# Attention, routed experts and a gated convolution FFN on one core: the first batch's rows and the late flag are taken earlier

## The chip, the core and the metric

The kernel runs on one core of one Trainium2 chip. The metric is the device time of one execution in microseconds (us), lower is better. An execution is timed as a whole; one execution is recorded by the hardware profiler, and its span (first to last instruction) is a little shorter than its own time.

## What is computed

Three stages, all in float32; the outputs of one are the inputs of the next.

```python
def reference(q_l, k_l, v_l, q_g, k_g, v_g, moe_*, moe2_*):
    # attention: 4 batches, 8 heads, 512 local rows with a window of 32, 32 global rows
    x = attention(...)                       # [4, 544, 512]
    # routed experts: 8 of them, one per row
    for b in range(4):
        for s in range(544):
            e = argmax(x[b, s] @ w_gate) or the row before's expert, by a local gate
            p = softmax(x[b, s] @ w_gate)
            y[b, s] = p[e] * (relu(x[b, s] @ w1[e]) @ w2[e])      # 512 -> 1024 -> 512
    # second FFN: 512 -> 1024, convolution of 3 taps along s, gate, 1024 -> 512
    h = relu(y @ w_in)
    c = conv3(h, conv_w)
    out = (h * sigmoid(c)) @ w_out
```

## The kernel before

**Stages.** The attention comes first. Its rows go to DRAM (`x_dram`), and the router sorts them by expert. The routed part then works in *slots*: slot `s` is up to 128 rows of one expert, gathered from `x_dram` by an indirect DMA and scattered to `y_dram` by another. 22 slots run: 0 and 1 in `fill`, 2 to 20 in `Moe.step` (L1280), 21 in `Moe.last` (L1190). Three more slots exist for other inputs, in a branch behind the last. The second FFN (`Ffn2.run`) then reads `y_dram` batch by batch, 8 units (blocks of 128 hidden columns) per batch.

**Arithmetic.** Every float32 factor is split into a high part and a low part, and each product is three matmuls: high x high, high x low, low x high. ScalarE makes the high part, VectorE subtracts it to get the low part. For activations these are `hi_t` (L1078/L1079: four transposes on TensorE, then the ScalarE copy) and `lo_t` (L1083); the tiles are `xh`/`xl` ahead of a first layer and `gh`/`gl` ahead of a second. For weights it is `Weights.split_k` (L1026/L1027: `wh`, `wl`). The weights of a slot's expert are split only where the expert changes (`resplit`, an `If` on a register).

**Order inside a step.** `step(s)` puts on TensorE: first layer of slot `s`, transposes of the rows `xs` of slot `s + 1`, second layer of slot `s - 1` (`l2_mm`, L1106), transposes of the hidden rows `hs` of slot `s`. Then `step(s + 1)` begins with its first layer (`l1_mm`, L1090). On VectorE: `xl`, the conversion of a piece of the second FFN's weights that is under way (`conv64`, L993 to L1000), the split of slot `s + 1`'s first-layer weights if its expert is new, the two `gl` of slot `s`, the split of second-layer weights if due. Every transpose group writes a PSUM buffer of the tag `tr`, of which there are two; so do `cwp` (L1166, transposed convolution weights) and `lf` (L946, the count behind the late flag). A buffer is free for the next group when its last reader is done, which for `hi_t` is `lo_t` on VectorE. Each engine takes its instructions in the order of the program.

**The end of the routed part.** `last(21)` mixes the first and second layers of the last slots with the split of the second FFN's input weights `W.f` (into the first-layer weight tiles), the loads of batch 0's rows (`load0`, L1331: five DMAs), their scaling by the router's probability (`scale0`, L1339) and transposes (`xt0`, L1346 to L1349), and ends with slot 21's copy from PSUM (L1259) and its scatter (L1063). Behind it every engine reads a flag into a register (L1178) and branches on it (L1179). The flag is not zero where a row of batch 0 lies in a slot so late that `load0` came before its scatter, or where more than 22 slots are needed; the branch then runs what is missing and loads, scales and transposes batch 0 again. Behind the branch the output weights are split and the second FFN starts.

**The second FFN's start.** TensorE's first layer of unit 0 and 1 (L1414), ScalarE's relu `f_hp` (L1438), convolution taps on ScalarE and VectorE (`fc`, L1431/L1433), gate (`fg`, L1449). Meanwhile SyncE loads rows of batch 1 (L1364: the global rows, then four times 128), which need all scatters; ScalarE scales the first 128 of them (L1370) in its order ahead of unit 1's `f_hp`.

```python
            rt.late_tokens(NSLOT - 4)            # L1685: NSLOT is 25
...
    def late_flag(self, n, t):                   # L944
        nc, f = self.nc, self.esi[:, 4, 1:2]
        nc.tensor.matmul(t, self.late, self.c.ones[:, 0:1], start=True, stop=True)
        nc.vector.tensor_scalar(f, self.esi[:, 4, 0:1], n - NA, None, ALU.is_gt)
        nc.vector.tensor_tensor(f, t, f, ALU.add)
```

Of the kernel before, what the change touches and what calls it, by code (L numbers as in the profile page):

```python
# [8 lines left out]
F32 = mybir.dt.float32  # L9
# [3 lines left out]
AF = mybir.ActivationFunctionType  # L13
ALU = mybir.AluOpType
# [3 lines left out]
P = 128  # L18
# [540 lines left out]
NSLOT = 25  # L559
NA = 2  # L560
# [413 lines left out]
SPLIT_W2 = {33: (0, 1, 2), 34: (3, 4, 5), 35: (6, 7)}  # L974
FILL = {1: 1, 3: 1, 6: 3, 7: 1, 8: 3, 9: 1, 10: 1, 11: 1, 12: 2, 13: 3, 15: 5, 16: 8}
HALF = 5
K_LAST = 2
N_GLOB = 6
N_GS = 4
N_Y = 24  # L980
PREP_F = ((3, 4, 5, 6), (1, 3, 5, 6), (1, 3, 5, 6))
PREP0 = {0: (0, 1, 12, 13), 3: (5, 2), 4: (6, 3), 5: (7, 4), 6: (8,), 7: (9,)}
POOL_L = ()
POOL_F = ()
DVE_F = (1, 3, 5, 7)
POOL_K = {1: (), 2: ()}


def conv64(nc, raw, out):
    hi, lo = raw[:, :, 1], raw[:, :, 0]  # L990
    v = nc.vector
    a = out.bitcast(I32)
    v.tensor_scalar(a, hi, 3, 0x7FFFFFFF, ALU.logical_shift_left, ALU.bitwise_and)  # L993
    v.scalar_tensor_tensor(a, hi, -2 ** 31, a, ALU.bitwise_and, ALU.bitwise_or)
    v.tensor_scalar(hi, hi, 1, 21, ALU.logical_shift_left, ALU.logical_shift_right)
    v.tensor_scalar(hi, hi, 897.0, -1.0, ALU.is_ge, ALU.mult)
    v.scalar_tensor_tensor(a, lo, 29, a, ALU.logical_shift_right, ALU.bitwise_or)
    v.tensor_scalar(lo, lo, 28, 1, ALU.logical_shift_right, ALU.bitwise_and)  # L998
    nc.gpsimd.tensor_tensor(a, a, lo, ALU.add)  # L999
    return lambda: v.scalar_tensor_tensor(a, a, 0x40000000, hi, ALU.bitwise_xor, ALU.bitwise_and)  # L1000


class Weights:
# [24 lines left out]

    def split(self, n, src, eng=None):
        for k in range(len(self.t[n])):  # L1030
            self.split_k(n, src, k, eng or (self.nc.gpsimd if k in POOL_K[n] else self.nc.vector))


class Moe:
# [134 lines left out]
    def run(self, cw6, cwr, cw, f2):  # L1169
        nc, W, tc = self.nc, self.W, self.tc  # L1170
        n = NSLOT - 3
        self.f2 = f2
        for s in range(NA, n - 1):
            self.step(s)
            if s == NA + 17:
                self.conv.append(conv64(nc, cw6, cwr))
        self.last(n - 1, cwr, cw)
        r = nc.values_load(self.rt.esi[0:1, 4, 1:2], min_val=0, max_val=P + 1)  # L1178
        with tc.If(r != 0):  # L1179
            r = nc.values_load(self.rt.esi[0:1, 4, 0:1], min_val=0, max_val=NB)  # L1180
            with tc.If(r > n - NA):
                for s in range(n, NSLOT):
                    self.slot(s)
                W.split(1, W.f)
            f2.load0()
            for i in range(5):
                f2.scale0(i, self.ps)
                f2.xt0(i, self.ps)
        for k in range(NFC):
            W.split_k(2, W.f, k, nc.gpsimd if k in POOL_F else nc.vector, nc.vector if k in DVE_F else None)  # L1190

    def last(self, s, cwr, cw):
        nc, W, f2 = self.nc, self.W, self.f2
        hp, hs = self.h_tile(), self.tp.tile([P, FF], F32, tag="hs", name="hs")
        xt, ht = self.xt.pop(s), {}
        w, y = W.t[1], {}
        ht = tuple(self.tp.tile([P, NFC, P], F32R, tag="g" + x, name="g" + x) for x in "hl")

        def split(a, b):
            for k in range(a, b):  # L1200
                W.split_k(1, W.f, k, nc.gpsimd if k in POOL_K[1] else nc.vector)

        def resplit(a, b):
            with self.tc.If(self.chg[s] != 0):
                for k in range(a, b):
                    W.split_k(2, W.s, k, nc.gpsimd if k in POOL_L else nc.vector)

        for k in range(K_LAST):
            self.l1_mm(xt, w, hp, k, range(2))
        split(0, K_LAST)  # L1210
        nc.scalar.activation(self.sig, self.sig, AF.Sigmoid)
        self.out(s - 1, self.l2(self.ht.pop(s - 1), W.t[2]))
        f2.load0()
        resplit(0, 4)
        for k in range(K_LAST, NKC - 1):
            self.l1_mm(xt, w, hp, k, range(2))
        self.conv_w(cwr, cw)
        self.rt.late_flag(s + 1, self.ps.tile([P, 4, P], F32, tag="tr", name="lf")[0:1, 0, 0:1])
        t = []
        for c in range(2):  # L1220
            self.l1_mm(xt, w, hp, NKC - 1, (c,))
            self.relu_c(hp, hs, c)
        for a in (0, 4):
            t.append(self.hi_t(hs, ht, a, self.ps))
        for a in (0, 4):
            self.lo_t(ht, a, t[a // 4])
        resplit(4, NFC)
        yp = self.y_tile()
        for k in range(NFC):
            self.l2_mm(ht, W.t[2], yp, k)  # L1230
            for f in PREP0.get(k, ()):
                if f < 10:
                    (f2.scale0 if f < 5 else f2.xt0)(f % 5, self.ps)
                else:
                    split(f - 10, f - 9)
        self.out(s, yp)

    def slot(self, s):
        nc, W = self.nc, self.W
# [37 lines left out]
        with self.tc.If(self.chg[s] != 0):  # L1277
            self.W.split(n, self.W.s, eng)

    def step(self, s):  # L1280
        W, hi = self.W, NSLOT - 3
        if NA < s <= NA + 16:
            self.raw_load(s - NA - 1)
        hs = self.relu(self.l1(self.xt.pop(s), W.t[1]))
        if s + 3 < hi:
            self.xs[s + 3] = self.gather(s + 3)
        self.xt[s + 1] = self.hi_lo_t(self.xs.pop(s + 1), NKC, "x")
        while self.conv:
            self.conv.pop()()
        self.resplit(s + 1, 1)  # L1290
        if s + 2 < hi:
            self.fetch(s + 1, 1)
        if s == NA:
            for _ in self.rest:
                pass
        else:
            self.out(s - 1, self.l2(self.ht.pop(s - 1), W.t[2]))
        self.ht[s] = self.hi_lo_t(hs, NFC, "g")
        self.resplit(s, 2)
        self.fetch(s, 2)  # L1300
        if NA < s <= NA + 16:
            self.convert(s - NA - 1)
# [15 lines left out]
class Ffn2:  # L1318
# [14 lines left out]
    def part0(self, i):  # L1333
        return (SG, 0, GT, 4) if i == 0 else (P, SG + P * i - P, i - 1, i - 1)

    def scale0(self, i, ps):
        n, _, j, a = self.part0(i)
        x = self.x_in[a][0:n]
        self.nc.vector.tensor_scalar(x, x, self.gate[0:n, j:j + 1], None, ALU.mult)  # L1339
# [227 lines left out]
def moe_kernel(ctx, tc, q_l, k_l, v_l, q_g, k_g, v_g, w_gate, w_local, w1, w2, w_in, conv_w, w_out, out):  # L1567
    nc = tc.nc
    outf = out.rearrange("b s d -> (b s) d")
    with tc.manual_schedule():  # L1570
# [90 lines left out]
        m, W, fill = todo["m"], todo["m"].W, todo["fill"]  # L1661
        xp = ctx.enter_context(tc.tile_pool(name="f_xp", bufs=1, reuse_waits="tile"))
        f2 = Ffn2(tc, xp, ident, y_dram, rt.gate, cw, W.t[1], W.t[2], outf)
        W.stage1(moe_ctx.enter_context(tc.tile_pool(name="w_y", bufs=1, reuse_waits="tile")))
        m.open(moe_ctx)
        with ExitStack() as c2:
            rp = c2.enter_context(tc.tile_pool(name="r_tb", bufs=1))
            rs = c2.enter_context(tc.tile_pool(name="r_ps", bufs=1, space=PSUM))
            m.fetch(0, 1)
            for i, y in enumerate(rt.phase_b(rp, lambda shape, name: rs.tile(shape, F32, tag="rt", name=name))):  # L1670
                if y == "idx":
                    for s in range(NA, NA + 3):
# [12 lines left out]
            rt.late_tokens(NSLOT - 4)  # L1685
        xa.close()
        W.ffn(moe_ctx.enter_context(tc.tile_pool(name="w_f", bufs=1)))
        m.run(cw6, cwr, cw, f2)
# [34 lines left out]
```

## Time and profile before

| | |
|---|---|
| three runs | 646.09, 648.47, 649.37 us; median 648.47 |
| the profiled execution | 645.35 us, its span 643.6 us |
| mean granted clock of TensorE | 0.995 of 2.4 GHz |
| busy in the span | TensorE 604.7 us (94%), VectorE 418.8 (65%), ScalarE 320.9 (50%), POOL 174.7 (27%) |

How to read the rows further down: PE is TensorE, DVE is VectorE, ACT is ScalarE, POOL is GpSimd, SP is SyncE; a "q" or "ld" behind the name is the engine's sequencer, or TensorE's weight loads. Times are us from the span's start unless marked ns. A timeline row has start, duration, engine, line, operation, output<-inputs, sizes, and how many like instructions it joins (x8); in brackets stands how long the engine sat idle before it and what released it. Matmuls are pipelined: the next one starts before the modelled end of the last.

### The profile page before, as it was taken

The page shows a single profiled execution, that of the slowest core. Times are in us where ns is not written, and L with a number is a line of the kernel's source. Part 1 is how long each engine was busy: PE and PEld are TensorE (multiplying, and loading weights), DVE is VectorE, ACT ScalarE, POOL GpSimd, SP SyncE. Part 2 cuts the span into 40 slices and gives each one's busy share as a digit, 9 for nine tenths or more (in the row PEclk, how much of TensorE's full clock was granted, in tenths as well). Part 3 has the DMA queues.
Part 4 walks back from the last instruction along what each step waited for, and adds up shares of the span by engine and source line. Part 5 has one row for each costly group of instructions (what it writes and reads, how often), then busy time and mean ns, then how long its engine had stood idle before and what let it go on. Part 6 is the DMA issues. An engine that isn't in the chain of part 4 may idle for free. (4 is left out here: it accounts for less than half of the span.)

```text
span 643.6 us, 15270 instructions
## 1 busy us (share of the span) xinstructions
PE 604.7 (94%) x5898; PEld 508.0 (79%) x5898; DVE 418.8 (65%) x874; ACT 320.9 (50%) x629; POOL 174.7 (27%) x226
## 2 busy tenths in 40 slices
PE   8888898888999999999999999987999999999997
PEld 7666676665778888888888888857998898898986
DVE  7877577958836676875778677586893393393340
ACT  4754555573225546352454634664874374373331
POOL 7664810070212232423222251000042042300200
PEclk9999999999999999999999999997999999999999
DMA  9999668652158454953545494023101201000001
GB/s 226 217 244 236 177 142 209 240 168 75 55 201 314 140 182 171 344 207 132 211 143 184 145 347 157 16 86 88 31 20 49 68 16 50 34 1 34 34 34 49
DMA packets 60089, 88.12 MB, mean 137 GB/s; under 512 B 25710, under 2 KB 34182, under 8 KB 59976
## 3 DMA queue, kind: packets, MB, share of 16 engines
q1 hardware_dynamic: 56488, 76.83, 38.3%
q0 software_dynamic: 3520, 10.23, 4.6%
q8 instruction: 48, 0.79, 0.5%
q14 instruction: 33, 0.27, 0.1%
HBM read 125.87 MB, written 15.79 MB: 220 GB/s over the span
## 5 line engine op out<-in xcount | busy, mean ns | idle before, releaser
L1433 DVE SCALAR_TENSOR_TENSOR fc<-f_hp,cw,fc 128x544 f32<-128x544 f32 (+2 forms) x66 | 51.4, 778 | 71.5 <-ACT fc L1431 70.0
L1027 DVE TENSOR_TENSOR wl<-ws,wh 128x512 fp32r<-128x512 f32 (+1 forms) x92 | 71.8, 848 | 5.3 <-ACT wh L1026 5.2
L1106 PE MATMUL yp<-wh,gh 128*128 128x512 f32 x176 | 71.0, 404 | 1.1 <-ACTq L1277 0.9
L1106 PE MATMUL yp<-wl,gh 128*128 128x512 f32 x176 | 69.0, 392 | 0.7 <-DVEq L1277 0.7
L1106 PE MATMUL yp<-wh,gl 128*128 128x512 f32 x176 | 69.1, 393 | 0.0
L1026 ACT CAST wh<-ws 128x512 fp32r<-128x512 f32 (+1 forms) x96 | 66.1, 779 | 0.0
L1255 ACT ACTIVATE hs<-hp 128x512 f32<-128x512 f32 x44 | 24.3, 595 | 74.2 <-PE hp L1090 74.1
L1090 PE MATMUL hp<-wh,xh 128*128 128x512 f32 x176 | 58.6, 405 | 0.7 <-ACT xh L1079 0.7
L1090 PE MATMUL hp<-wl,xh 128*128 128x512 f32 x176 | 56.2, 392 | 0.0
L1090 PE MATMUL hp<-wh,xl 128*128 128x512 f32 x176 | 56.0, 391 | 0.0
L1491 PE MATMUL f<-wh,fh 128*128 128x512 f32 (+1 forms) x144 | 55.5, 385 | 0.0
L1491 PE MATMUL f<-wl,fh 128*128 128x512 f32 (+1 forms) x144 | 55.0, 382 | 0.0
L1491 PE MATMUL f<-wh,fl 128*128 128x512 f32 (+1 forms) x144 | 55.0, 382 | 0.0
L1063 POOL DMA_INDIRECT y_dram<-ys,sidx x22 | 24.6, 1118 | 105.7 <-ACT ys L1259 88.9
L1083 DVE TENSOR_TENSOR gl<-hlp,gh 128x512 fp32r<-128x512 f32 x44 | 28.4, 686 | 32.4 <-ACT gh L1079 32.3
L278 ACT ACTIVATE pr<-sp,nm 128x128 f32<-128x128 f32 x128 | 36.6, 376 | 25.7 <-DVE nm L275 25.7
L999 POOL TENSOR_TENSOR wf<-wf,fx 128x512 int32<-128x512 int32 x16 | 20.8, 1303 | 100.9 <-DVE fx L998 100.9
L1259 ACT COPY ys<-yp 128x512 f32<-128x512 f32 x22 | 12.9, 587 | 61.2 <-PE yp L1106 56.5
L1051 POOL DMA_INDIRECT xs<-x_dram,gidx x22 | 27.5, 1249 | 45.5 <-ACT pr L278 34.0
L1106 PEld LDWEIGHTS yp<-wh,gh 128*128 128x128 f32 x176 | 33.1, 188 | 7.7 <-ACTq L1277 1.1
L1090 PEld LDWEIGHTS hp<-wl,xh 128*128 128x128 f32 x176 | 32.9, 188 | 7.8 <-DVE wl L1027 0.9
L1106 PEld LDWEIGHTS yp<-wh,gl 128*128 128x128 f32 x176 | 33.0, 188 | 7.6 <-DVE gl L1083 0.6
(357 smaller groups left out, 1492.5 us busy)
## 6 DMA issues: line engine op xcount, KB each, us to landing
ws<-in_moe_w_dram SPq DMA_DIRECT2D x42, 2048.0 KB
fx<-y_dram SPq DMA_DIRECT2D x17, 256.0 KB
raw<-in_k_l_dram SPq DMA_DIRECT2D x16, 256.0 KB
x_dram<-x SPq DMA_DIRECT2D x16, 256.0 KB
fx<-in_moe_w_in_dram SPq DMA_DIRECT2D x8, 512.0 KB
fx<-in_moe_w_out_dram SPq DMA_DIRECT2D x8, 512.0 KB
out_dram<-fy SPq DMA_DIRECT2D x16, 256.0 KB
VA<-in_v_l_dram SPq DMA_DIRECT2D x20, 192.0 KB
```

Of the source, the lines that this page charges most:

```text
L278: nc.scalar.activation(pr[:, hp, :], sp[:, hp, :], AF.Exp, bias=nm[:, hp:hp + 1], scale=-1.0)
L999: nc.gpsimd.tensor_tensor(a, a, lo, ALU.add)
L1026: (cp.tensor_copy if cp else self.nc.scalar.copy)(h, src[n][:, k, :])
L1027: eng.tensor_tensor(l, src[n][:, k, :], h.bitcast(F32), ALU.subtract)
L1051: self.nc.gpsimd.indirect_dma_start(out=xs, out_offset=None, in_=self.x_dram[0:n, :], in_offset=bass.IndirectOffsetOnAxis(ap=self.rt.gidx[ ...
L1063: self.nc.gpsimd.indirect_dma_start(out=self.y_dram[:, :], out_offset=bass.IndirectOffsetOnAxis(ap=self.rt.sidx[:, s:s + 1], axis=0), in_= ...
L1083: self.nc.vector.tensor_tensor(hl[1][:, a:a + 4], t, hl[0][:, a:a + 4].bitcast(F32), ALU.subtract)
L1090: self.nc.tensor.matmul(hp[c], a[:, k, :], b[:, 512 * c:512 * c + 512], start=k == 0 and m == 0, stop=k == NKC - 1 and m == 2)
L1106: self.nc.tensor.matmul(yp, a[:, k, :], b, start=k == 0 and m == 0, stop=k == NFC - 1 and m == 2)
L1255: self.nc.scalar.activation(hs[:, 512 * c:512 * c + 512], hp[c], AF.Relu)
L1433: nc.vector.scalar_tensor_tensor(c[:, a:b], hp[:, a + t:b + t], self.cw[:, t, f:f + 1], c[:, a:b], ALU.mult, ALU.add)
L1491: self.nc.tensor.matmul(yp[:, cs], x[:, c], w[:, cs], start=f == 0 and n == 0, stop=f == NFC - 1 and n == 2)
```

## The change

The rows of batch 0 in slots 19 and later now count as late (21 and later before). So `load0` goes out at the start of step 20, behind slot 18's scatter, instead of behind slot 20's second layer. The five `scale0` stand in front of `last`, the five `xt0` inside slot 21's first layer instead of its second. In `last` the first layer runs in one piece, the second layer of slot 20 holds the transposes of slot 21's hidden rows, and slot 20's copy stands behind the split of slot 21's second-layer weights. The late flag is computed behind step 17, as are the registers behind step 18; a second value (flag not zero) goes to TensorE's sequencer as a hint on where the branch will go. The convolution weights are converted one step earlier and transposed in step 20 instead of the last slot. Slot 21's result is copied into a buffer of the second FFN, and its scatter stands behind the branch (and once inside it).

```diff
-            self.step(s)
-            if s == NA + 17:
+            if s == n - 2:
+                f2.load0()
+            self.step(s, (cwr, cw) if s == n - 2 else None)
+            if s == NA + 15:
+                self.rt.late_flag(n, self.ps.tile([P, 4, P], F32, tag="tr", name="lf")[0:1, 0, 0:1])
+                f = self.rt.esi[:, 4, 1:3]
+                nc.vector.tensor_scalar(f[:, 1:2], f[:, 0:1], 0, None, ALU.not_equal)
+            if s == NA + 16:
+                self.flag = nc.values_load(f[0:1, 0:1], min_val=0, max_val=P + 1)
+                self.hint = nc.values_load(f[0:1, 1:2], engines=[mybir.EngineType.PE], min_val=0, max_val=1)
                 self.conv.append(conv64(nc, cw6, cwr))
-        self.last(n - 1, cwr, cw)
-        r = nc.values_load(self.rt.esi[0:1, 4, 1:2], min_val=0, max_val=P + 1)
-        with tc.If(r != 0):
+        for i in range(5):
+            f2.scale0(i)
+        y = self.last(n - 1)
+        with tc.If(self.flag != 0, label="late"):
+            self.scatter(n - 1, y)
+            nc.vector.memset(self.rt.sidx[:, n - 1:n], 4 * P * NT)
             r = nc.values_load(self.rt.esi[0:1, 4, 0:1], min_val=0, max_val=NB)
...
+        self.scatter(n - 1, y)
         for k in range(NFC):
...
-    def last(self, s, cwr, cw):
+    def last(self, s):
         nc, W, f2 = self.nc, self.W, self.f2
...
+        for k in range(NKC):
+            self.l1_mm(xt, W.t[1], hp, k, range(2))
+            for i in PREP0[k]:
+                f2.xt0(i, self.ps)
...
+        for c in range(2):
+            self.relu_c(hp, hs, c)
+        for k in range(2):
+            W.split_k(1, W.f, k, v)
...
+        yp, hp = self.y_tile(), self.ht.pop(s - 1)
         for k in range(NFC):
...
+            self.l2_mm(hp, W.t[2], yp, k)
+            if k in (1, 2):
+                t = self.hi_t(hs, ht, 4 * k - 4, self.ps)
+                self.lo_t(ht, 4 * k - 4, t)
+        with self.tc.If(self.chg[s] != 0):
+            W.split(2, W.s, v)
+        self.out(s - 1, yp)
+        for k in range(2, NKC):
+            W.split_k(1, W.f, k, v)
+        self.tc.mark_branch_hint_location("late", self.hint, engines=[mybir.EngineType.PE])
+        yp = self.l2(ht, W.t[2])
+        y = f2.x_in[3]
+        nc.scalar.copy(y, yp)
+        return y
...
-    def step(self, s):
+    def step(self, s, cw=None):
...
-            self.out(s - 1, self.l2(self.ht.pop(s - 1), W.t[2]))
+            yp, ht = self.y_tile(), self.ht.pop(s - 1)
+            for k in range(NFC):
+                self.l2_mm(ht, W.t[2], yp, k)
+                if k == 3 and cw:
+                    self.conv_w(*cw)
+            self.out(s - 1, yp)
...
-            rt.late_tokens(NSLOT - 4)
+            rt.late_tokens(NSLOT - 6)
```

`PREP0` is now `((), (0, 1), (2,), (3, 4))`: which `xt0` follow which quarter of the first layer. Lines shift a little by the change; in the three pieces below the changed kernel's L1074 is L1078 of before, L1079 is L1083, L1086 is L1090, L1102 is L1106, L1023 is L1027, L1059 is L1063 and L1271 is L1277.

TensorE from the end of step 17 into the first layer of slot 18, before:

```order
L1106 MATMUL yp<-wh_7_2746,gh 128x512
L1106 MATMUL yp<-wl_7_2747,gh 128x512
L1106 MATMUL yp<-wh_7_2746,gl 128x512
L1078 MATMUL hlp<-ident,hs 128x128 x8
L1277 UNCONDITIONAL_BRANCH
L1090 MATMUL hp<-wh_0_2724,xh 128x512 x2
L1090 MATMUL hp<-wl_0_2725,xh 128x512 x2
```

and with the change:

```order
L1102 MATMUL yp<-wh_7_2746,gl 128x512
L1074 MATMUL hlp<-ident,hs 128x128 x8
L1271 UNCONDITIONAL_BRANCH
L946 LDWEIGHTS late
L946 MATMUL lf<-c_ones,late 1x1
L1086 MATMUL hp<-wh_0_2724,xh 128x512 x2
L1086 MATMUL hp<-wl_0_2725,xh 128x512 x2
```

The count `lf` now stands between the transposes of slot 17's hidden rows and the first layer of slot 18; it stood in the last slot. Its buffer is that of the first four transposes.

VectorE in step 20, from the split of slot 21's first-layer weights on, with the change:

```order
L1271 COMPARE_AND_BRANCH
L1023 TENSOR_TENSOR wl_0_2725<-ws_3452,wh_0_2724 128x1024
L1023 TENSOR_TENSOR wl_1_2727<-ws_3452,wh_1_2726 128x1024
L1023 TENSOR_TENSOR wl_2_2729<-ws_3452,wh_2_2728 128x1024
L1023 TENSOR_TENSOR wl_3_2731<-ws_3452,wh_3_2730 128x1024
L1271 UNCONDITIONAL_BRANCH x2
L1163 COPY cw<-cwp 128x24
L1079 TENSOR_TENSOR gl<-hlp,gh 128x512 x2
```

The copy of `cwp` is new here; before, `gl` followed the four `wl` directly. In step 17 the same four `wl` (of slot 18) stand ahead of the two `gl` in both kernels.

POOL from slot 20's scatter to the second FFN, with the change:

```order
L1059 DMA y_dram<-ys,sidx 2176x512
L1184 COMPARE_AND_BRANCH
L1059 DMA y_dram<-fx,sidx 2176x512
...
L1184 UNCONDITIONAL_BRANCH
L1184 ISA
L1184 UNCONDITIONAL_BRANCH
L1059 DMA y_dram<-fx,sidx 2176x512
L1356 MEMSET f_hp_7519 128x1
```

L1184 is the branch on the flag; its two upper rows of `fx` are inside it and behind it. Before, both scatters stood ahead of the branch.

## Rows read from the trace of the kernel before

**Rows 1.** part 2 of the page: granted clock in 40 slices
```profile
PEclk9999999999999999999999999997999999999999
```

**Rows 2.** waits of TensorE, 371 to 466 us: total, times, longest
```profile
PE f L1414 <- PEq L1179: 4.2, 1, 4.2
...
PE f_tr L1379 <- DVE fxl L1381: 0.9, 1, 0.9
```

**Rows 3.** TensorE's timeline, end of step 17: start, duration, what
```profile
371.80 1.04 PE L1078 MATMUL hlp<-ident,hs 128*128 128x128 f32 x8
372.59 0.72 PE L1090 MATMUL hp<-wh,xh 128*128 128x512 f32 x2
```

**Rows 4.** VectorE's timeline, the same place
```profile
372.06 4.62 DVE L1027 TENSOR_TENSOR wl<-ws,wh 128x1024 fp32r<-128x1024 f32 x4
376.60 1.28 DVE L1083 TENSOR_TENSOR gl<-hlp,gh 128x512 fp32r<-128x512 f32 x2
```

**Rows 5.** two stretches: us, busy by engine, then the granted clock
```profile
437.12:443.95 6.83, 5.68 (x25) 5.71 (x26) 5.12 (x10) 2.18 (x4) 0.28 (x6) 0.50 0.55 145
443.95:447.10 3.15, 3.15 (x27) 3.15 (x26) 2.87 (x5) 2.11 (x4) 0.00 (x0) 1.00 0.39 120
```

**Rows 6.** TensorE's timeline, end of step 20 to the branch
```profile
409.75 0.72 PE L1090 MATMUL hp<-wh,xh 128*128 128x512 f32 x2
...
412.60 0.39 PE L1106 MATMUL yp<-wh,gh 128*128 128x512 f32 x1
...
418.04 0.62 PE L1090 MATMUL hp<-wh,xh 128*128 128x512 f32 x2
...
419.66 0.16 PE L946 MATMUL lf<-c_ones,late 128*1 128x1 bf16 x1
...
428.75 0.60 PE L1346 MATMUL f_tr<-ident,fx 128*128 128x128 f32 x4
...
433.40 0.63 PE L1346 MATMUL f_tr<-ident,fx 128*128 128x128 f32 x4
```

**Rows 7.** VectorE's timeline: step 20, last slot, after the branch
```profile
405.60 4.63 DVE L1027 TENSOR_TENSOR wl<-ws,wh 128x1024 fp32r<-128x1024 f32 x4
...
414.02 1.23 DVE L1027 TENSOR_TENSOR wl<-wf,wh 128x1024 fp32r<-128x1024 f32 x1 [0.15 <-ACT wh L1026]
...
424.60 2.49 DVE L1027 TENSOR_TENSOR wl<-ws,wh 128x512 fp32r<-128x512 f32 x4
...
438.73 0.69 DVE L1027 TENSOR_TENSOR wl<-wf,wh 128x512 fp32r<-128x512 f32 x1 [3.36 <-ACT wh L1026]
...
445.61 1.69 DVE L1433 SCALAR_TENSOR_TENSOR fc<-f_hp,cw,fc 128x544 f32<-128x544 f32 x2
```

**Rows 8.** ScalarE's timeline, last slot's copy and second FFN
```profile
434.55 0.59 ACT L1259 COPY ys<-yp 128x512 f32<-128x512 f32 x1
...
445.71 0.73 ACT L1370 ACTIVATE fx<-fx,gate 128x512 f32<-128x512 f32 x1 [0.21 <-DMA fx<-y_dram]
447.10 0.63 ACT L1438 ACTIVATE f_hp<-f 128x544 f32<-128x544 f32 x1 [0.66 <-PE f L1414]
```

**Rows 9.** POOL's timeline, the scatters of slots 20 and 21
```profile
419.10 0.97 POOL L1063 DMA_INDIRECT y_dram<-ys,sidx  x1 [8.00 <-ACT ys L1259]
435.41 0.97 POOL L1063 DMA_INDIRECT y_dram<-ys,sidx  x1 [15.34 <-DVE f_x0l L1349]
```

**Rows 10.** SyncE's timeline, the two loads of y rows
```profile
422.59 2.23 SPq L1331 DMA_DIRECT2D fx<-y_dram  x5
438.09 2.84 SPq L1364 DMA_DIRECT2D fx<-y_dram  x5
```

**Rows 11.** the branch behind the last slot, TensorE's sequencer, ns
```profile
L1179 PEldq COMPARE_BRANCH  x1: 3768/3768/3768, 434.1 to 434.1; - x1
```

**Rows 12.** chain that ended last, by time, 433 to 466 us
```profile
438.27 8.80 PE f L1414 x48
...
464.75 0.66 PE f_tr L1379 x4
```

More of the change, by code (lines that the diff above doesn't have):

```diff
@@ L976 @@
 HALF = 5
-K_LAST = 2
 N_GLOB = 6
@@ L981 @@
 PREP_F = ((3, 4, 5, 6), (1, 3, 5, 6), (1, 3, 5, 6))
-PREP0 = {0: (0, 1, 12, 13), 3: (5, 2), 4: (6, 3), 5: (7, 4), 6: (8,), 7: (9,)}
-POOL_L = ()
-POOL_F = ()
+PREP0 = ((), (0, 1), (2,), (3, 4))
 DVE_F = (1, 3, 5, 7)
-POOL_K = {1: (), 2: ()}
 def conv64(nc, raw, out):
@@ L1030, in split @@
         for k in range(len(self.t[n])):
-            self.split_k(n, src, k, eng or (self.nc.gpsimd if k in POOL_K[n] else self.nc.vector))
+            self.split_k(n, src, k, eng or self.nc.vector)
 class Moe:
@@ L1186, in run @@
             for i in range(5):
-                f2.scale0(i, self.ps)
+                f2.scale0(i)
                 f2.xt0(i, self.ps)
+        self.scatter(n - 1, y)
         for k in range(NFC):
-            W.split_k(2, W.f, k, nc.gpsimd if k in POOL_F else nc.vector, nc.vector if k in DVE_F else None)
-    def last(self, s, cwr, cw):
+            W.split_k(2, W.f, k, nc.vector, nc.vector if k in DVE_F else None)
+    def last(self, s):
         nc, W, f2 = self.nc, self.W, self.f2
-        hp, hs = self.h_tile(), self.tp.tile([P, FF], F32, tag="hs", name="hs")
-        xt, ht = self.xt.pop(s), {}
-        w, y = W.t[1], {}
-        ht = tuple(self.tp.tile([P, NFC, P], F32R, tag="g" + x, name="g" + x) for x in "hl")
[L1199 to L1211, printed above, removed]
-        self.out(s - 1, self.l2(self.ht.pop(s - 1), W.t[2]))
[L1213 to L1228, printed above, removed]
-        for k in range(NFC):
[L1230 to L1236, printed above, removed]
@@ new lines, in last @@
+        v = nc.vector
+        nc.scalar.activation(self.sig, self.sig, AF.Sigmoid)
+        xt, hp = self.xt.pop(s), self.h_tile()
+        for k in range(NKC):
+            self.l1_mm(xt, W.t[1], hp, k, range(2))
+            for i in PREP0[k]:
+                f2.xt0(i, self.ps)
+        hs = self.tp.tile([P, FF], F32, tag="hs", name="hs")
+        for c in range(2):
+            self.relu_c(hp, hs, c)
+        for k in range(2):
+            W.split_k(1, W.f, k, v)
+        ht = tuple(self.tp.tile([P, NFC, P], F32R, tag="g" + x, name="g" + x) for x in "hl")
@@ L1296, in step @@
         else:
-            self.out(s - 1, self.l2(self.ht.pop(s - 1), W.t[2]))
+            yp, ht = self.y_tile(), self.ht.pop(s - 1)
[4 more added lines that the diff above has]
+            self.out(s - 1, yp)
         self.ht[s] = self.hi_lo_t(hs, NFC, "g")
@@ L1334, in part0, with scale0 @@
         return (SG, 0, GT, 4) if i == 0 else (P, SG + P * i - P, i - 1, i - 1)
-    def scale0(self, i, ps):
+    def scale0(self, i):
         n, _, j, a = self.part0(i)
```

## The prediction

> **What bounds the kernel now.** I read the clock line first, then the waits of TensorE, then the timelines of each engine around every place the diff touches, and last the chain of waits. The clock line is full in every slice but one, the 28th [rows 1]. From 371 to 466 us TensorE waits for others little: its two stops that matter are 4.24 us in front of the second FFN and 0.88 us in front of the transposes at 464.75 us [rows 2, 12]. So through the routed slots the kernel lasts as long as TensorE's own instructions. What any of them waits is added to the end, unless a later wait of TensorE shrinks by as much.
>
> Around the branch it is otherwise. TensorE's matmuls of the last slot end at 434.03 us (433.40 + 0.63), and the next matmul is the second FFN's at 438.27 [rows 6, 12]. Behind that gap the clock is 0.50 (1.2 GHz) from 437.12 to 443.95: 25 matmuls are busy for 5.68 us there, where 27 take 3.15 right behind it [rows 5]. At full clock 25 would take 25/27 x 3.15 = 2.92 us, so the fall costs 2.8. The chain then runs through 48 matmuls in 8.80 us and ScalarE's `f_hp` of the second unit at 447.10 into a loop of ScalarE and VectorE, which releases TensorE's transposes at 464.75; from there TensorE sets the end [rows 8, 12]. What is gained at that 447.10 comes out at the end.
>
> **Step 17, the flag's early matmul: +4.8 us.** The matmul `lf` itself is cheap (0.16 us [rows 6]). Its place is not. It now stands on TensorE behind the eight transposes of `hs` and ahead of the first layer of slot 18. It takes the next buffer of the transposes' PSUM pair, which is free only when VectorE has made the first `gl` from it. In step 17 VectorE stands at another job: slot 18 starts a new expert, and the four `wl` of its first-layer weights run from 372.06 to 376.68; `gl` follows at 376.60, two in 1.28, so the first is done at 376.60 + 0.64 = 377.24 [rows 4]. Before, nothing on TensorE waited for this: the first layer began at 372.59, straight behind the transposes [rows 3]. TensorE takes its matmuls in order, so slot 18's first layer and all behind it now start at about 377.24 + 0.16 = 377.4, which is 4.8 us late. VectorE has no other work that fills this later, and TensorE has no wait from here to slot 20 that could shrink.
>
> A page of the Trainium skill, "TensorE: Matmul & The Clock Gate" (section "Architectural detail"), says that TensorE's queue can pull weight loads ahead of matmuls in flight. If that held for matmuls, the stall would be nothing and the time 644.8; it is said of weight loads only, and no row here shows a matmul that passed a waiting one.
>
> **The clock in step 17: +2.8 us, or nothing.** From the end of the transposes (371.80 + 1.04 = 372.84 [rows 3]) to 377.24 TensorE idles 4.4 us. The trace has one idle of that length, 4.24 us, and the clock fell; idles of 0.9 us show no fall [rows 1, 2]. So I take the fall, at the 2.8 us worked out above. It may not come, since TensorE was dense ahead of this gap: lower end 0. If the half clock lasts as long as it did and all of it is work, it costs half of 6.83 = 3.4 us [rows 5]: upper end.
>
> **Step 20, the conv weights' transpose: +1.2 us, inside the next term.** `cwp` takes one of the same two buffers, so the second four transposes of `hs` wait until VectorE has copied it out, and that copy stands behind the four `wl` that end at 405.60 + 4.63 = 410.23 [rows 7]. Slot 21's first layer then starts at about 410.95 instead of 409.75 [rows 6].
>
> **The last slot and the start of the second FFN: -3.7 us.** Worked from before's own durations, without the shift of step 17. First layer: 2 x (412.60 - 409.75) = 5.70. Five groups of input transposes, one small: about 5 x 0.35 = 1.77 (four in 0.36 by 428.75 to 429.11, where the next matmul starts). Second layer of slot 20: 418.04 - 412.60 = 5.44 [rows 6]. Eight transposes of `hs` 0.8 [rows 3], and about 0.5 of waiting for ScalarE's relus. So slot 20 ends at 410.95 + 14.2 = 425.2. Slot 21's second layer is then paced by VectorE, whose eight `wl` at 2.49/4 = 0.62 [rows 7] begin only behind the `gl` at about 425.4 and end at 430.4; three matmuls later it is 431.1, and ScalarE's copy of 0.59 ends at 431.7. Before it ended at 434.55 + 0.59 = 435.14 [rows 8].
>
> VectorE still has two `wl` of 1.23 [rows 7], so the second FFN could start near 432.9 instead of 438.27. But that isn't what counts. The rows of slot 21 must be scattered before SyncE loads the second batch, and ScalarE scales its first 128 rows ahead of the second `f_hp`. By before's rows: scatter 0.27 behind the copy (435.41 - 435.14), 2.68 until the loads are issued (438.09 - 435.41), 7.62 until the scaling starts (445.71 - 438.09), 0.73 for it [rows 8 to 10]. 431.7 + 0.27 + 2.68 + 7.62 + 0.73 = 443.0; I add 0.4 for slot 20's scatter, which now starts only some 3 us ahead (its landing took up to 422.59 - 419.10 = 3.49 [rows 9, 10]). That gives 443.4 against 447.10: 3.7 us. The 48 matmuls from 432.9 on end by 441.7 even at before's 8.80, so neither branch nor clock counts at this place any more. Bounds: 2 us, if slot 21 ends a microsecond later and its rows land in 3.5; 7 us if the loads came early enough and only VectorE's split of the output weights bound (438.73 to 445.61 is 6.9 [rows 7], from about 433 to 440).
>
> **At nothing:** the five early loads (they need the rows of slot 18, two slots back; behind them on SyncE stands only the load of slot 21's second-layer weights, which waits for the splits of slot 20 anyway), the five scalings (five short instructions on VectorE behind the `gl` of step 20, while TensorE has the 5.7 us of the first layer ahead; without that cover they would delay the first transposes by about what they take), the scatter behind the branch (POOL has nothing else, and its wait is in the sum), the early registers (TensorE's sequencer reads them beside matmuls), the removed scaling waits of TensorE (inside the sum above), the branch hint. The hint removes at best the 3.77 us that TensorE's sequencer spends in the branch [rows 11], and the loads cover these; if it doesn't work, the 48 matmuls start at 431.1 + 3.8 and end at 443.7, 0.3 us behind the loads. The skill's "Advanced Engine Details and Errata" (section "Control Flow Timing") gives about 108 ns for a compare-and-branch. By that figure the branch would never have cost anything; this trace's 3768 ns decides, and the sum is the same by both.
>
> **Sum.** +4.8 + 2.8 - 3.7 = +3.9 us. The profiled execution took 645.35 us (span 643.6), so it would take 649.3. The median of the runs shown is 648.47, 3.1 above the profiled one; on it the forecast is **652.4 us**.
>
> **Rivals.**
> - *The clock holds in step 17.* All else as above: 648.47 + 4.8 - 3.7 = 649.6, no measurable change. For it: TensorE is dense up to 372.84, which it was not ahead of 434. Against it: the gap is longer than the one at which it fell. It decides at 372.84 to 377.24, nowhere else.
> - *Faster: `lf` doesn't wait.* If `gl` came before the `wl`, or the buffer were another, the step-17 terms would go: 648.47 - 3.7 = 644.8. It decides at whether the first `gl` is done by 372.8. Against it: the order of VectorE is unchanged there, and its row says 377.24.
> - *A second fall.* The loop of the second FFN now starts less early than TensorE could, so TensorE waits some 3 us more ahead of the transposes that stood at 464.75. With a fall there, 652.4 + 2.8 = 655.2.
> - *The reload.* With a row of batch 0 in slot 19 or 20, the branch is taken and loads, scales and transposes again, some 7.6 us by the loads alone: 660. By the reference's router at its fixed seed, slots 18 to 20 hold expert 6, to which batch 0 sends four rows, which all come first, in slot 18. So it hardly comes.
>
> **How the numbers follow.** A measurement of this kernel can tell about 0.5% from no change, 3.2 us here. Chances: forecast 0.50, with its own range 651.0 to 654.0; second fall 0.10; clock holds 0.27; no wait 0.09; reload and what I don't see 0.04. Slower by over 0.5% (above 651.7): the forecast but for its lower part where the last slot gains over 4.4 us (0.40), the second fall (0.09) and the reload (0.03): 0.52. Faster (below 645.2): no wait, and a little of the clock that holds with a gain near 7: 0.10. The same: 0.38. The range leaves out most of the no-wait case and the reload: 646.3 (clock holds, gain 7) to 656.0.
>
> **What would show it.** Right: in the changed trace TensorE idles 4 to 5 us ahead of slot 18's first layer, released through `gl` (named VectorE, or `lf`); the granted clock there is 0.5 for some 6 us; step 18 and all behind stand 7 to 8 us later; the copy of slot 21 ends some 4 us later than 435.1 and the second `f_hp` stands near 451, released by the scaled rows; no 3.8 us of branch on the chain. Wrong: slot 18's first layer within 1 us of 372.6; or a second FFN that starts at once and sets the loop itself.

## The result and the profile after

The changed kernel took 655.55 us in the median of 8 runs, the kernel before 648.0 in the median of 8 beside it. The ratio is 1.0115 with a 95% interval of 1.0088 to 1.0142, that is 5.7 to 9.2 us slower. One run of the changed kernel took 3306.18 us, for a reason that nothing here shows; ratios leave it out, as they do every run over 1.5% above the fastest of its kernel (four of the twelve in experiment 4, two of the 30 of before beside experiments 3, 5, 7 and 8), and medians are of all runs. The forecast was 652.4 (646.3 to 656.0): the sign and the range held, the size (+3.9 on 648.47) was too small.

The execution profiled took 654.88 us (span 653.1), 9.5 us more in the span than before. Of these, 3.0 us have nothing to do with the change. Step 17's transposes already begin at 374.84 instead of 371.80, because in this execution the clock fell twice in the attention, whose code is the same in both kernels; the first slot's first layer, right behind it, is already 3.0 us late (145.83 against 142.81). The clock line shows it in the fifth and the ninth slice; the 24th is step 17's:

```profile
PEclk9999899989999999999999979999999999999999
```

The profiles of the experiments show one to four such slices in the attention or the first slots, at changing places, and that of before none. They probably make up much of the 6 us by which runs of one kernel spread (before: 645.44 to 651.54). So below, stretches are compared by their own lengths, and times only by medians and ratios.

TensorE's longest waits from 360 to 480 us (total, times, longest), to be read beside [rows 2]:

```profile
PE lf L946 <- DVE gl L1079: 4.5, 1, 4.5
PE f L1413 <- ACT f_hp L1437: 3.6, 1, 3.6
PE f L1413 <- PEq L1184: 2.5, 1, 2.5
PE f_tr L1378 <- DVE fxl L1380: 1.7, 1, 1.7
PE hlp L1074 <- DVE xl L1079: 0.7, 1, 0.7
PE hlp L1074 <- DVE cw L1163: 0.5, 1, 0.5
```

Four of these waits were in no row of before. The first is step 17's. TensorE's timeline there, beside [rows 3]:

```profile
374.84 1.03 PE L1074 MATMUL hlp<-ident,hs 128*128 128x128 f32 x8
380.37 0.16 PE L946 MATMUL lf<-c_ones,late 128*1 128x1 bf16 x1 [4.50 <-DVE gl L1079]
380.47 1.22 PE L1086 MATMUL hp<-wh,xh 128*128 128x512 f32 x2
...
388.18 0.60 PE L1074 MATMUL hlp<-ident,xs 128*128 128x128 f32 x4
```

Slot 18's first layer begins 380.47 - 374.84 = 5.63 us behind the first transpose; before it was 0.79. That is +4.84 us. It then lasts 388.18 - 380.47 = 7.71 us, where it lasted 5.86 (by the place of the next transposes, 378.45 before): +1.85 us, at half clock. The two stretches of the fall and of the rise behind it (columns as in [rows 5]):

```profile
378.10:384.93 6.83, 4.56 (x12) 3.50 (x12) 6.16 (x13) 0.00 (x0) 0.85 (x2) 0.51 0.80 300
384.95:388.20 3.25, 3.25 (x16) 2.62 (x15) 0.00 (x0) 0.00 (x0) 1.68 (x2) 0.99 1.01 407
```

The clock is at 0.5 for as long as it was in front of the second FFN (6.83 us), but it fell at about 378.2, and TensorE idled until 380.37. So 2.1 us of the half clock cost nothing, where 1.15 did in before.

Steps 19 and 20, TensorE's timeline, then VectorE's and POOL's in step 19:

```profile
407.74 0.66 PE L1074 MATMUL hlp<-ident,hs 128*128 128x128 f32 x4 [0.75 <-DVE xl L1079]
...
421.57 0.71 PE L1086 MATMUL hp<-wh,xh 128*128 128x512 f32 x2
```

```profile
404.84 1.30 DVE L990 SCALAR_TENSOR_TENSOR cwr<-cw,cwr 24x128 int32<-24x128 int32 x1
```

```profile
404.69 1.30 POOL L995 TENSOR_TENSOR wf<-wf,fx 128x512 int32<-128x512 int32 x1 [8.48 <-DVE fx L994]
```

Slot 21's first layer begins at 421.57, 11.82 us later than before's 409.75 [rows 6]; at step 18's transposes the delay was 388.18 - 378.45 = 9.73. Of the 2.1 us between, 1.0 came in step 19 and 1.1 in step 20 (step 20's first transposes stand at 413.74 against 403.03).

The other end of the change, slot 21's copy and what follows it. ScalarE's timeline, beside [rows 8]:

```profile
442.07 0.59 ACT L1229 COPY fx<-yp 128x512 f32<-128x512 f32 x1 [1.42 <-issue]
...
455.98 0.72 ACT L1369 ACTIVATE fx<-fx,gate 128x512 f32<-128x512 f32 x1 [6.82 <-DMA fx<-y_dram]
456.61 0.61 ACT L1437 ACTIVATE f_hp<-f 128x544 f32<-128x544 f32 x1
```

POOL's, beside [rows 9] (the first row is a scatter of step 17, for comparison):

```profile
376.40 1.92 POOL L1059 DMA_INDIRECT y_dram<-ys,sidx  x1 [0.30 <-ACT gh L1075]
...
421.19 0.99 POOL L1059 DMA_INDIRECT y_dram<-ys,sidx  x1 [11.72 <-ACT ys L1253]
439.03 4.69 POOL L1059 DMA_INDIRECT y_dram<-ys,sidx  x1 [16.86 <-ACT ys L1253]
446.42 1.18 POOL L1059 DMA_INDIRECT y_dram<-fx,sidx  x1 [2.70 <-DVE wh L1022]
```

VectorE's at the same time, and SyncE's loads, beside [rows 7, 10]:

```profile
435.71 4.90 DVE L1023 TENSOR_TENSOR wl<-ws,wh 128x512 fp32r<-128x512 f32 x8
440.52 2.36 DVE L1023 TENSOR_TENSOR wl<-wf,wh 128x1024 fp32r<-128x1024 f32 x2
445.00 0.69 DVE L1023 TENSOR_TENSOR wl<-wf,wh 128x512 fp32r<-128x512 f32 x1 [2.12 <-ACT wh L1022]
```

```profile
449.04 2.78 SPq L1363 DMA_DIRECT2D fx<-y_dram  x5
```

The reader is to see three distances. Slot 21's copy ends at 442.66, but its scatter begins at 446.42: 3.76 us, forecast with 0.67. That last row names VectorE, but slot 20's scatter landed 6.5 us after its start, at about 445.5, and slot 21's begins 0.9 us behind that. In experiment 4 the distance from landing to scatter is the same 0.9, and the row names the landing. The loads are issued 449.04 - 446.42 = 2.62 us later (forecast 2.68), and the scaling starts 455.98 - 449.04 = 6.94 us behind them (7.62). The second `f_hp` at 456.61 is 9.51 us later than before's 447.10; at the transposes of step 18 the delay was 9.73. So everything from step 18 to the second FFN's loop gave back 0.2 us, not 3.7. From the second `f_hp` to the end of the span it is 196.5 us in both executions (643.6 - 447.10 and 653.1 - 456.61), so a delay there comes out whole at the end, as the prediction had it.

### The profile page after: what moved, and what is told of

Read it like the earlier page. It is cut to its first block, busy times and chain, and to the rows that moved or that the text cites. A ratio compares the mean times of both kernels' runs of the same rounds, so it can differ in the third digit from the quotient of the medians.

```text
span 653.1 us, 15267 instructions
## 1 busy us (share of the span) xinstructions
PE 607.9 (93%) x5898; PEld 509.9 (78%) x5898; DVE 420.4 (64%) x875; ACT 320.5 (49%) x629; POOL 180.2 (28%) x226
## 5 line engine op out<-in xcount | busy, mean ns | idle before, releaser
L1023 DVE TENSOR_TENSOR wl<-ws,wh 128x512 fp32r<-128x512 f32 (+1 forms) x92 | 71.7, 847 | 1.3 <-ACT wh L1022 1.3
L1102 PE MATMUL yp<-wh,gh 128*128 128x512 f32 x176 | 71.0, 403 | 0.9 <-ACTq L1271 0.9
L1102 PE MATMUL yp<-wl,gh 128*128 128x512 f32 x176 | 69.1, 392 | 0.8 <-DVEq L1271 0.7
L1102 PE MATMUL yp<-wh,gl 128*128 128x512 f32 x176 | 69.0, 392 | 0.0
L1086 PE MATMUL hp<-wh,xh 128*128 128x512 f32 x176 | 59.4, 412 | 0.7 <-ACT xh L1075 0.7
L1059 POOL DMA_INDIRECT y_dram<-ys,sidx x21 | 29.3, 1396 | 109.4 <-ACT ys L1253 107.1
L1086 PE MATMUL hp<-wl,xh 128*128 128x512 f32 x176 | 56.8, 397 | 0.0
L1086 PE MATMUL hp<-wh,xl 128*128 128x512 f32 x176 | 56.3, 394 | 0.0
L1079 DVE TENSOR_TENSOR gl<-hlp,gh 128x512 fp32r<-128x512 f32 x44 | 28.5, 686 | 33.1 <-ACT gh L1075 30.1
L1086 PEld LDWEIGHTS hp<-wh,xh 128*128 128x128 f32 x176 | 31.9, 191 | 11.5 <-issue 5.2
L1086 PEld LDWEIGHTS hp<-wl,xh 128*128 128x128 f32 x176 | 33.5, 191 | 7.8 <-DVE wl L1023 0.5
L1086 PEld LDWEIGHTS hp<-wh,xl 128*128 128x128 f32 x176 | 33.5, 190 | 7.5 <-DVE xl L1079 0.2
```

Source lines behind the costliest of these rows:

```text
L1023: eng.tensor_tensor(l, src[n][:, k, :], h.bitcast(F32), ALU.subtract)
L1059: self.nc.gpsimd.indirect_dma_start(out=self.y_dram[:, :], out_offset=bass.IndirectOffsetOnAxis(ap=self.rt.sidx[:, s:s + 1], axis=0), in_= ...
L1079: self.nc.vector.tensor_tensor(hl[1][:, a:a + 4], t, hl[0][:, a:a + 4].bitcast(F32), ALU.subtract)
L1086: self.nc.tensor.matmul(hp[c], a[:, k, :], b[:, 512 * c:512 * c + 512], start=k == 0 and m == 0, stop=k == NKC - 1 and m == 2)
L1102: self.nc.tensor.matmul(yp, a[:, k, :], b, start=k == 0 and m == 0, stop=k == NFC - 1 and m == 2)
```

## The experiments

All are changes of the kernel named, with nothing left out of the computation. Each stands beside runs of the kernel before on the same chip. Not all ran on one chip, so two experiments are compared by their ratios as well.

### 1. The count in another buffer

```diff
             if s == NA + 15:
-                self.rt.late_flag(n, self.ps.tile([P, 4, P], F32, tag="tr", name="lf")[0:1, 0, 0:1])
+                self.rt.late_flag(n, self.y_tile()[0:1, 0:1])
```

> The changed kernel with the count's matmul in a PSUM buffer of the second layer's output pair (free by then) instead of the transposes' pair; its place on TensorE stays. Theory (the wait for gl is the loss, and the clock falls because of it): TensorE's idle of 4.5 us and the 0.5 clock at slot 18's first layer go; 655.5 - 4.8 - 1.9 = about 649, between 648 and 650. Rival (the other parts of the change cost it, such as the early flag reads or the moved loads): above 653.

649.54 us (before 647.81; ratio 1.0009, 0.9986 to 1.0032). TensorE's waits, 360 to 470 us:

```profile
PE f L1413 <- ACT f_hp L1437: 4.0, 1, 4.0
PE f L1413 <- PEq L1184: 2.6, 1, 2.6
PE hlp L1074 <- DVE xl L1079: 0.7, 1, 0.7
PE hlp L1074 <- DVE cw L1163: 0.5, 1, 0.5
```

The wait for `gl` is gone and nothing stands in its place; the time fell by 6 us. With this one buffer exchanged, the rest of the change is worth nothing that can be told from noise (a loss of 2.1 to a gain of 0.9 us), which is still not the 3.7 us forecast for it.

### 2. That part alone, in the kernel before

```diff
             self.step(s)
+            if s == NA + 15:
+                self.rt.late_flag(n, self.ps.tile([P, 4, P], F32, tag="tr", name="lf")[0:1, 0, 0:1])
...
-        self.rt.late_flag(s + 1, self.ps.tile([P, 4, P], F32, tag="tr", name="lf")[0:1, 0, 0:1])
```

> The kernel before with one part of the change alone: the late flag's count and its two small VectorE instructions stand behind step 17, in the transposes' pair, and nothing else moves. Theory: +4.8 of waiting and +1.9 to +2.8 of half clock, so 648.0 + 6.7 to 7.6 = 654.7 to 655.6, with TensorE idle 4.5 us behind gl. Rival (the wait is absorbed before the end): within 1 us of 648.

653.14 us, ratio 1.0072 (1.0045 to 1.0098): +4.7 us, 2.9 to 6.4. TensorE's timeline in step 17:

```profile
376.50 1.03 PE L1078 MATMUL hlp<-ident,hs 128*128 128x128 f32 x8
382.03 0.16 PE L946 MATMUL lf<-c_ones,late 128*1 128x1 bf16 x1 [4.50 <-DVE gl L1083]
382.12 0.99 PE L1090 MATMUL hp<-wh,xh 128*128 128x512 f32 x2
...
389.31 0.60 PE L1078 MATMUL hlp<-ident,xs 128*128 128x128 f32 x4
```

The same wait of 4.50 us, and 389.31 - 382.12 = 7.19 us for the first layer, 1.33 more than before. Wait and clock come to 6.2 us in this profile. The time rose less than the expected 6.7 to 7.6, which lies above the interval; the interval just reaches the 6.2. So the rival, a wait absorbed before the end, is out, and most of the wait reaches the end.

### 3. The count one step earlier

```diff
-            if s == NA + 15:
+            if s == NA + 14:
```

> The changed kernel with the late flag's count one step earlier, behind step 16, in the transposes' pair as in the changed kernel. Slot 17 has slot 16's expert, so no wl of a first layer stand ahead of gl there. Theory (the length of the wait is VectorE's split): TensorE waits only 1.0 to 1.3 us for gl, the clock doesn't fall there, and the time is 655.5 - 3.5 - 1.9 = about 650. Rival (the wait is that of the count itself or of the flag's chain): again 4 to 5 us, 655.

650.59 us, ratio 1.0022 (0.9997 to 1.0048). The wait, from TensorE's waits (350 to 475 us):

```profile
PE lf L946 <- DVE gl L1079: 1.1, 1, 1.1
```

It is 1.1 us where no expert changes, and the clock is full there. So the 4.5 us are VectorE's four `wl`, as the forecast had it, and not the count.

### 4. Why the end of the routed part gave nothing: slot 20's scatter

In the changed kernel, POOL's scatter of slot 20 takes 4.69 us (others 1 to 2), and slot 21's scatter starts only when it has landed. Experiment 1 with the last two splits of the input weights behind the branch:

```diff
         self.scatter(n - 1, y)
+        for k in range(2, NKC):
+            W.split_k(1, W.f, k, nc.vector)
         for k in range(NFC):
...
         self.out(s - 1, yp)
-        for k in range(2, NKC):
-            W.split_k(1, W.f, k, v)
```

> As lf_other_buffer, and the last two splits of the second FFN's input weights (on ScalarE and VectorE) stand behind the branch instead of ahead of it, so VectorE is idle from the end of slot 21's eight wl on. In the changed kernel POOL's scatter of slot 20 takes 4.7 us where the others take 1.0, and slot 21's scatter waits for its landing. Theory (VectorE's row of subtractions holds up POOL's writing of the scatter): the scatter of slot 20 ends about 0.8 us behind VectorE's last wl, some 2.3 us earlier than before relative to slot 21's copy; the second f_hp 1.5 to 2.3 us earlier, so about 2 us below lf_other_buffer. Rival (POOL's own work around the branch holds the scatter): it still takes 4 to 5 us, and the time is that of lf_other_buffer or above it.

646.50 us, ratio 0.9942 (0.991 to 0.9974): 3 us less than experiment 1 by the medians, 4.3 by the ratios. Its twelve runs spread from 640.21 to 653.57, so the size is uncertain. VectorE's, POOL's and ScalarE's timelines:

```profile
431.20 4.89 DVE L1023 TENSOR_TENSOR wl<-ws,wh 128x512 fp32r<-128x512 f32 x8
441.40 1.23 DVE L1023 TENSOR_TENSOR wl<-wf,wh 128x1024 fp32r<-128x1024 f32 x1 [5.30 <-ACT wh L1022]
```

```profile
434.53 2.42 POOL L1059 DMA_INDIRECT y_dram<-ys,sidx  x1 [16.86 <-ACT ys L1253]
441.08 0.97 POOL L1059 DMA_INDIRECT y_dram<-fx,sidx  x1 [4.14 <-DMA y_dram<-ys,sidx]
```

```profile
451.66 0.61 ACT L1437 ACTIVATE f_hp<-f 128x544 f32<-128x544 f32 x1
```

and experiment 1's second `f_hp`, where slot 20's scatter began at 435.76 and took 4.69 us:

```profile
453.77 0.60 ACT L1437 ACTIVATE f_hp<-f 128x544 f32<-128x544 f32 x1
```

The scatter ends at 434.53 + 2.42 = 436.95, which is 0.86 us behind VectorE's last `wl` (431.20 + 4.89 = 436.09). In the changed kernel it ended at 439.03 + 4.69 = 443.72, which is 0.84 behind its last one there (440.52 + 2.36 = 442.88). POOL's branch stands 0.2 us ahead of the scatter in both, so it is not what held it, and ScalarE ran nothing from 434.25 to 437.56 in experiment 4, while the scatter was held; the end of VectorE's row is what moved.

The page "SBUF — State Buffer" of the Trainium skill (section "SBUF: two separate sides") tells of a lock that fits in part: VectorE and GpSimd share a pair of ports, and a VectorE instruction with two SBUF inputs, against a GpSimd instruction that reads SBUF, holds it for its whole length if it starts first. The same section of the Trainium skill says that GpSimd can't write the descriptors of its DMAs while it is locked out, but says so of VectorE instructions in a two-port mode. Each `wl` has two SBUF inputs. A lock of one instruction alone does not explain a wait over several of them to the end of the row, and in step 17 the scatter at 376.40 took 1.92 us in the middle of such a row. Why it got in between two subtractions there and not here is open.

The second part of the expectation missed. The second `f_hp` comes 451.66 - 434.53 = 17.13 us behind the start of slot 20's scatter, in experiment 1 it was 453.77 - 435.76 = 18.01: 0.9 us sooner, not 1.5 to 2.3. The scatter landed 5.6 us after its start, which is 3.2 behind POOL's end, where it was 1.8 in the changed kernel; why isn't shown. So the end of POOL's work follows VectorE's row, but only 0.9 us of the gain is seen in this profile, and the rest is open.

### 5. Slot 20's copy first

```diff
+        self.out(s - 1, yp)
         with self.tc.If(self.chg[s] != 0):
             W.split(2, W.s, v)
-        self.out(s - 1, yp)
```

> split_behind with slot 20's copy and scatter ahead of the split of slot 21's second-layer weights instead of behind it. Theory (VectorE's subtractions hold up POOL's writing): the scatter starts 2 us earlier, but ends again only about 0.8 us behind the last of VectorE's eight wl, so it takes over 4 us, and the time is not better than split_behind (646.5). Rival (it was the branch on POOL that held it): it takes 1.0 us, lands some 2 us earlier, and slot 21's scatter and the second f_hp come 2 us earlier.

649.18 us, ratio 1.0 (0.9976 to 1.0025): 2.7 us worse than experiment 4 by the medians, 3.8 by the ratios. VectorE, POOL and ScalarE:

```profile
434.94 4.90 DVE L1023 TENSOR_TENSOR wl<-ws,wh 128x512 fp32r<-128x512 f32 x8 [1.48 <-ACT wh L1022]
```

```profile
434.66 0.97 POOL L1059 DMA_INDIRECT y_dram<-ys,sidx  x1 [14.84 <-ACT ys L1253]
442.14 0.97 POOL L1059 DMA_INDIRECT y_dram<-fx,sidx  x1 [6.50 <-ACTq L1184]
```

```profile
441.28 0.59 ACT L1229 COPY fx<-yp 128x512 f32<-128x512 f32 x1 [2.73 <-issue]
...
453.93 0.63 ACT L1437 ACTIVATE f_hp<-f 128x544 f32<-128x544 f32 x1 [1.30 <-PE f L1413]
```

Neither expectation came as told. The copy waits for slot 20's second layer, ScalarE splits later behind it, and so VectorE's row starts only at 434.94, 0.28 us behind the scatter's start, which therefore runs free in 0.97. This doesn't tell the two theories apart. It shows that slot 21's scatter starts right behind its copy (441.28 + 0.59, then 442.14) once slot 20's rows are down, and that the second `f_hp` then waits for TensorE and not for the rows, and comes sooner: 12.06 us behind the copy, where it was 13.51 in experiment 4. That gain went into the copy, which is 1.5 us later (counted from step 17's scatter), as TensorE waits 1.2 us for ScalarE's split. What else made the time worse than experiment 4's isn't seen in the two profiles.

### 6. Without the hint

```diff
-                self.hint = nc.values_load(f[0:1, 1:2], engines=[mybir.EngineType.PE], min_val=0, max_val=1)
...
-        self.tc.mark_branch_hint_location("late", self.hint, engines=[mybir.EngineType.PE])
```

> As lf_other_buffer, without the branch hint, its value and its register. Theory (the hint does nothing for this branch: TensorE's sequencer spent 3.5 us in it with the hint and 3.8 in the kernel before): the branch takes 3.4 to 3.8 us and the time is within 0.5 us of lf_other_buffer. Rival (the hint shortens it a good deal): the branch takes over 4.5 us; the time still moves little, since the loads release the second f_hp.

648.98 us, ratio 1.0017 (0.9992 to 1.0041), the same as experiment 1. The branch on TensorE's sequencer, in ns, with the hint (experiment 1) and without:

```profile
L1184 PEldq COMPARE_BRANCH  x1: 3527/3527/3527, 437.4 to 437.4; - x1
```

```profile
L1183 PEldq COMPARE_BRANCH  x1: 3737/3737/3737, 437.3 to 437.3; - x1
```

The hint takes off 0.2 us, if anything: over all kernels of this study the branch took 3.49 to 4.09 us in the seven with the hint (besides experiment 9's 1.98, where TensorE has other work meanwhile), and 3.67 to 3.95 in the four without it. In the trace the hint stands behind step 18 on TensorE, 228 matmuls ahead of its branch; whether it would do more beside it wasn't tried. "Runtime: NRT & Kernel Launch" of the Trainium skill (section "Instruction fetch mechanics") says that a taken branch out of the fetched pages waits for a fetch of its target. The 3.5 to 4.1 us on TensorE, against some 0.05 on the other engines, fit that, but no run here tells a fetch from another cause.

### 7. The convolution weights at their old step

```diff
+            if s == NA + 17:
                 self.conv.append(conv64(nc, cw6, cwr))
...
-        t = self.ps.tile([P, 4, P], F32, tag="tr", name="cwp")[:, 0, 0:3 * NFC]
+        t = self.y_tile()[:, 0:3 * NFC]
```

> split_behind with the conversion of the convolution weights back at its old step and their transpose in a PSUM buffer of the second layer's pair. Theory: TensorE's waits of 0.7 us (xl, step 19) and 0.5 us (cw, step 20) go and nothing takes their place: 646.5 - 1.2 = 645.3. Rival (VectorE or ScalarE are late at the same place): the waits move to another tile and the time stays.

This is on top of experiment 4: 645.46 us, ratio 0.9937 (0.9909 to 0.9965). The waits for `xl` and `cw` are gone from TensorE's list; the 1 us between the medians is within the spread, and the ratios agree.

### 8. The rows scaled two units later

Experiments 1 and 7 (without 4), and:

```diff
-                if b + 1 < B and f < 4:
-                    x2[b + 1, f] = self.scaled(xs.pop((b + 1, f)), 4 * b + 4 + f + (b + 1) // 2,
+                d = f if b else f - 2
+                if b + 1 < B and 0 <= d < 4:
+                    x2[b + 1, d] = self.scaled(xs.pop((b + 1, d)), 4 * b + 4 + d + (b + 1) // 2,
                                                 self.nc.gpsimd if b else None)
```

> lf_other_buffer with the conversion of the convolution weights back at its old step, their transpose in a PSUM buffer of the second layer's pair, and the scalings of batch 1's rows on ScalarE two units later, so that they no longer stand ahead of the second unit's f_hp. Theory (the loads behind slot 21's scatter hold the loop only through ScalarE's order): the waits of 0.7 and 0.5 us in steps 19 and 20 go, the second f_hp follows TensorE's units and VectorE's split of the output weights, 3 to 5 us earlier; 649.5 - 1.2 - 4 = about 644. Rival (the rows are needed so soon that the wait only moves): 648 to 649.

643.14 us, ratio 0.9908 (0.9887 to 0.993): 6 us faster than before, the best kernel of the study with the next one. ScalarE's timeline:

```profile
433.93 0.59 ACT L1230 COPY fx<-yp 128x512 f32<-128x512 f32 x1 [1.44 <-issue]
...
445.87 0.63 ACT L1438 ACTIVATE f_hp<-f 128x544 f32<-128x544 f32 x1 [1.68 <-PE f L1414]
...
450.45 0.71 ACT L1370 ACTIVATE fx<-fx,gate 128x512 f32<-128x512 f32 x1
```

The second `f_hp` now waits for TensorE, 445.87 - 434.52 = 11.35 us behind slot 21's copy (456.61 - 442.66 = 13.95 in the changed kernel). Slot 20's scatter takes 4.69 us as ever, and it no longer matters. How much of the 6 us comes from the convolution weights and how much from the scaling, no run separates; experiment 7 puts the former at 1 us or less.

### 9. TensorE kept busy through the branch

```diff
         nc.scalar.copy(y, yp)
+        self.warm(12)
```

> scale_later with twelve matmuls of no use (their result is read by nothing) behind slot 21's second layer, ahead of the branch, so that TensorE is not idle while its sequencer is in the branch. In scale_later TensorE idles 3.1 us there, the clock falls behind it, and the second FFN's first units run at half clock while they hold the loop. Theory (the fall costs about 2.8 us there): no fall, the second f_hp 2 to 3 us earlier, 643.1 - 2 = about 641. Rival (the clock falls anyway, or VectorE's split of the output weights holds the loop as soon as TensorE doesn't): 642.5 to 644.

642.70 us, ratio 0.9928 (0.9905 to 0.9952), not to be told from experiment 8. TensorE's timeline and ScalarE's:

```profile
433.24 2.88 PE L1056 MATMUL wm<-wh 128*128 128x512 f32 x12
436.57 0.36 PE L1415 MATMUL f<-f_x0h,wh 128*128 128x272 f32 x1 [0.45 <-PEq L1185]
```

```profile
433.48 0.59 ACT L1230 COPY fx<-yp 128x512 f32<-128x512 f32 x1 [1.36 <-issue]
...
442.85 0.63 ACT L1439 ACTIVATE f_hp<-f 128x544 f32<-128x544 f32 x1 [1.58 <-PE f L1415]
```

The clock stays full, and the second `f_hp` comes 442.85 - 434.07 = 8.78 us behind the copy, 2.6 us sooner. The time hardly shows it (about 641 was expected): VectorE is in the split of the output weights until its first taps at 443.78, and TensorE now waits 1.3 us for scaled rows of batch 1. That is the rival's second half.

### 10. The later scaling in the kernel before

The edit of experiment 8 alone, in the kernel before.

> The kernel before with one edit alone: batch 1's rows are scaled on ScalarE two units later. Theory (there the second f_hp waits for TensorE's units at half clock, not for the rows): within 1 us of before, so what scale_later gained needs the earlier end of the routed part. Rival (the scalings themselves cost the loop): 1.5 to 3 us faster than before.

649.79 us, ratio 1.0037 (1.0008 to 1.0066): no gain, rather a loss of 0.5 to 4.3 us. There the second `f_hp` waited for TensorE anyway [rows 8]. So the later scaling gains nothing by itself; what experiment 8 gained needs the change's earlier end of the routed part.

## Why the prediction was right, and where it was off

- **Step 17, +4.8 us: right.** 4.84 measured, released by `gl`. Experiments 1, 2 and 3 take it away, bring it into the kernel before, and shrink it to 1.1 us by the place alone. That nothing later fills it was right as well.
- **The clock, +2.8 us: right that it fell, too dear.** 1.85 us in this profile, 1.33 in experiment 2. The price was taken from a fall of which 1.15 us lay in idle time; here 2.1 did.
- **Step 20, +1.2 us: right, 1.1; but 1.0 more in step 19.** What was overlooked is that the conversion of the convolution weights moved one step earlier, where VectorE still converts the last piece of the second FFN's weights. `xl` comes late there, and TensorE waits 0.75 us; the forecast had no term for it. One of VectorE's small instructions takes 1.30 us there, beside a POOL instruction that began 0.15 us earlier and ends 0.15 us earlier (0.28 us in before, at 399.70). That alone is longer than the wait; no run separates it.
- **The last slot, -3.7 us: wrong, 0.2.** The working from slot 21's first layer to its copy held in its total: 442.66 - 421.57 = 21.1 us, forecast 431.7 - 410.95 = 20.75. The step that failed is "I add 0.4 for slot 20's scatter". It took a scatter's price from two that POOL wrote in 1 us, and no scatter of before took over 1.92. Moved behind the split, slot 20's starts in the middle of ten subtractions in a row and takes 4.69, and slot 21's waits 3.1 us longer than forecast. With the 0.9 that steps 19 and 20 took above their term and the 0.3 of the working, that is 4.3; the loads and their landing came 0.8 sooner than forecast, which leaves the 3.5 us of difference.
- **The sum.** Forecast +3.9, by medians +7.5 (5.7 to 9.2). From the places above it is 4.84 + 1.85 - 0.2 = 6.5.
- **The range: partly luck.** The forecast's own range, 651.0 to 654.0, was missed. Its terms at their worst (4.8 + 3.4 - 2.0) give 654.7; 655.55 lies within 656.0 only by the room that the rival of a second fall (655.2) gave. What used that room up was a last slot that gained nearly nothing, where the bounds were 2 to 7 us.
- **"At nothing"** fits for the registers, the loads, the five scalings and the hint: TensorE's list of waits has none of them but the branch, 2.5 us of wait (3492 ns with the hint), and the wait for `f_hp` behind it is longer. The rival of a second fall came true in another place: TensorE waits 3.56 us for the second `f_hp`, and the clock is at half from about 457 to 460. It cost nothing that shows, as the 196.5 us from that `f_hp` to the end are those of before.

## What to carry to other kernels

A one-element matmul that is moved to where its value is free can cost as much as a layer: look at what last reads the buffer that it takes, and what that reader's engine does just then. A scatter by POOL is not a constant: here it took from 0.97 to 4.69 us, by what VectorE ran beside it. And where an engine works in order, as ScalarE here, a wait for rows that are needed only two units later belongs two units later; it paid once the routed part ended earlier, and not in the kernel before.

## What was not expected of the hardware

- An indirect scatter that starts under a long row of VectorE's subtractions ended 0.84 to 0.86 us behind the last of them in the last slot, whether that made it 2.42 or 4.69 us long. In step 17 one got in between after 1.92 us.
- A hint to TensorE's sequencer, given 228 matmuls ahead of the branch, left 3.53 us of branch where it was 3.74 without; over all kernels the two kinds overlap.
- A VectorE instruction of 0.28 us took 1.30 us beside a POOL instruction of the same length that had begun just ahead of it.
